# A planner that writes the issue order gets new costs, waits and port rules

## Chip, core and metric

The kernel runs on one core of one Trainium2 chip. The metric is the device time of one execution in microseconds (us). Five instruction streams work side by side on the core: TensorE (PE, matrix products), VectorE (DVE), ScalarE (ACT), GpSimd (POOL) and SyncE (SP, which here only issues DMA transfers). Each stream is worked off in the order in which it was written; an instruction that has to wait holds up everything behind it in its stream.

## The reference, cut to what matters

```python
kv  = einsum('bhsd,bhse->bhde', k, v)             # 4 batches, 8 heads, 576 tokens, 64 wide
x   = einsum('bhsd,bhde->bhse', q, kv)
x   = x / sqrt(mean(x*x, -1) + 1e-6) * g_norm     # -> 2304 tokens x 512
h   = x @ w_in                                    # 512 x 2048
y   = (h * tanh(softplus(h))) @ w_out             # 2048 x 512
h2  = y @ w2_in                                   # 512 x 1024
s   = h2 * softmax(h2)
out = layer_norm(s) * g_ln @ w2_out               # 1024 x 512
```

## The kernel before

The 2304 tokens stand in six blocks of 384 (b = 0 to 5), each with three tiles of 128 rows (r = 0 to 2). Every product is made of fp16 parts, a high and a low one, in three passes. The float data come as 64-bit words that the core decodes itself: one **piece** of a weight matrix (512 KB, 48 pieces: `("1", 0..15)` of w_in, `("2", 0..15)` of w_out, then `"3"` and `"4"` of the second layer) is loaded into one of five staging slots (`ld`, SP), scaled (`sc`, ACT, L598), has its sign taken out (`sg`, POOL, L603), is put together (`low`, `put`, DVE, L608 and L615) and split into high and low (`whi`, ACT, L626; `wlo`, DVE, L633 or L635). A slot is free for the fifth next piece when `put` is through.

The stages on TensorE are: k^T v of a batch (`kv`, L307); queries times that (`xo`, L482, in block 0 L352); `H`, the first product of the first layer (L738, units of 12 matmuls; L833 from block 3 on); `Y`, the second (L907, units of 12); the first product of the second layer (`"2"`, L1012, seven products for each pair of token tiles p = 0 to 8) and its second (`O`, L1148, likewise seven products of 12 matmuls).

Between `xo` and `H` a tile goes through `sq` (ACT), `ms` (DVE), `rho` (POOL, a power: L507 and L509), `xf` (DVE, L515), `xhi` (ACT), `xlo` (DVE); blocks 0 and 1 are then transposed on TensorE (`xP`, L460), the others by a DMA (`xT`, L539). Queries of blocks 2 to 5 come by `ldq` (SP, L281, into one buffer, so the next block's load waits until the last one's queries are used), `qhi`, `qlo`, and a transposing DMA `qT` (L434; three buffers, so each waits for the `xo` of the tile three before it). Queries of blocks 0 and 1 are transposed on TensorE (`qT`, L338 and L442).

A softmax tile of the second layer goes `ex` (ACT, L1049), `z` (DVE, L1055), `sq2` (ACT, L1060), `den` and `pw` (POOL, L1066 to L1076), `ln` (ACT, L1082), then `hi` (ACT, L1118), `lo` (DVE, L1124), and a transposing DMA (L1129). Out of the `O` bank, `e1`, `e2`, `e7` (ACT, L1159) keep partial products, `c12` (ACT, L1172) and `c11`, `c22`, `c21` (DVE, L1167) make the output rows.

None of this order is written out. Each step is a task with an engine, a cost in us, what it comes after, and a lag. `Plan.order` (list scheduling by due times) lays the tasks out, `Plan.search` tries 300 random changes of due times and keeps the order whose last TensorE task ends first; that order is then emitted. Where the plan leaves a gap on TensorE, the emitting loop puts dummy products (`keep_warm`, L1663, `idle<-ident` or `hp<-ident`), one for each 0.12 us of the gap less a constant:

```python
            if not heated and gap > 1.0:
                keep_warm(int((gap - 0.4) / 0.12), warm)
            elif gap > 0.5 and at_time < 150 and done.issuperset(h_free[h_line[0]]):
                keep_warm(int((gap - 0.2) / 0.12), h_open(h_line[0]))
```

The dummies read `ident`, which GpSimd writes at the start (L1676, L1677) beside two clears of buffers (L1681, L1682).

Of the kernel before, what the change touches and what calls it, by code (L numbers as in the profile page):

```python
# [142 lines left out]
def tile_attn_moe_moe2(  # L143
# [1036 lines left out]
    def task(key, engine, cost, fn, args, after=(), lag=0.1, due=None):  # L1180
# [9 lines left out]
    LAND, PAIR, QLD, PIECE = 2.0, 2.15, 3.0, 1.6  # L1190
# [3 lines left out]
    def far_group(kind, j):  # L1194
# [5 lines left out]
        for w, which in enumerate("rt"):  # L1200
            if w:
                for n in range(4):
                    after = [los["r", m] for m in range(parts[0])] if n == 0 else []
# [4 lines left out]
            for n in range(parts[w]):  # L1208
# [14 lines left out]
    for n, u in enumerate(PIECES):  # L1223
# [27 lines left out]
        task(("wlo", u), "V", 0.77 if scaled else 0.72, w_lo, (u,), [("whi", u)])  # L1251
# [23 lines left out]
    for b in range(B):  # L1275
        for i in range(4):
# [7 lines left out]
            task(("ld", b, i), "S", PAIR, load_pair, (b, i), free, LAND)  # L1284
# [10 lines left out]
    for c in range(4):  # L1295
        task(("lq0", c), "S", QLD / 4, load_q0, (c,), (), LAND)
# [441 lines left out]
```

## Time and profile before

| | |
|---|---|
| time, median of 3 runs (lowest, highest) | 594.47 us (593.57, 595.64) |
| profiled execution: time, span from first to last instruction | 594.5 us, 592.6 us |
| TensorE busy, matmuls | 581.6 us, 98% of the span, 4818 |
| VectorE, ScalarE, GpSimd busy | 428.3, 369.6, 138.7 us |
| DMA moved | 82.30 MB, mean 139 GB/s |
| chain that ended last: TensorE, DMA, ScalarE | 88%, 6%, 3% |

The span is what the trace covers; the time is that of the same execution as the runs measure it. A busy TensorE may be busy with dummies, which the page does not tell apart from work.

### The profile page before, as it was taken

The page shows a single profiled execution, that of the slowest core. Times are in us where ns is not written, and L with a number is a line of the kernel's source. Part 1 is how long each engine was busy: PE and PEld are TensorE (multiplying, and loading weights), DVE is VectorE, ACT ScalarE, POOL GpSimd, SP SyncE. Part 2 cuts the span into 40 slices and gives each one's busy share as a digit, 9 for nine tenths or more (in the row PEclk, how much of TensorE's full clock was granted, in tenths as well). Part 3 has the DMA queues.
Part 4 walks back from the last instruction along what each step waited for, and adds up shares of the span by engine and source line. Part 5 has one row for each costly group of instructions (what it writes and reads, how often), then busy time and mean ns, then how long its engine had stood idle before and what let it go on. Part 6 is the DMA issues. An engine that isn't in the chain of part 4 may idle for free.

```text
span 592.6 us, 12017 instructions
## 1 busy us (share of the span) xinstructions
PE 581.6 (98%) x4818; PEld 405.2 (68%) x4818; DVE 428.3 (72%) x722; ACT 369.6 (62%) x633; POOL 138.7 (23%) x180
## 2 busy tenths in 40 slices
PE   8899998999999999999999999999999999999997
PEld 6676665666666667877877778775455567767786
DVE  1587777887556858898775787887666888778751
ACT  4568555773646544455556765765767768888651
POOL 1526443320412530000100010000433115253300
PEclk9899999999999999999999999999999999999999
DMA  8982884997775440001342632607063329977695
GB/s 292 306 274 72 215 195 96 279 240 213 180 167 127 71 54 2 1 19 72 106 127 76 199 127 80 234 1 283 1 125 58 68 51 211 177 151 137 119 207 141
DMA packets 128423, 82.30 MB, mean 139 GB/s; under 512 B 94320, under 2 KB 115824, under 8 KB 128368
## 3 DMA queue, kind: packets, MB, share of 16 engines
q1 hardware_dynamic: 128208, 81.55, 54.9%
q8 instruction: 37, 0.61, 0.4%
q14 instruction: 18, 0.15, 0.1%
q10 hardware_dynamic: 160, 0.00, 0.0%
HBM read 46.67 MB, written 12.06 MB: 99 GB/s over the span
## 4 chain that ended last, share of the span: by engine, by line
PE 88%; DMA 6%; ACT 3%; DVE 1%; issue 1%; POOL 1%; SPq 0%; POOLq 0%; ACTq 0%
PE y L907 29%; PE hp L833 14%; PE h L1012 14%; PE op L1148 13%; PE hp L738 13%; DMA qraw<-in_q_dram 3%; PE kvp L307 2%; PE xo L482 1%; DMA st<-in_moe_w_in_dram 1%; DMA st<-in_moe_w_out_dram 1%; PE qTp L442 1%; PE qTp L338 1%; ACT g L884 1%; ACT w L626 0%; ACT qhl L421 0%
## 5 line engine op out<-in xcount | busy, mean ns | idle before, releaser
L907 PE MATMUL y<-g,w 128*128 128x384 f16 x1152 | 201.5, 326 | 1.5 <-ACT yT L927 1.5
L907 PEld LDWEIGHTS <-w 128*128 128x128 f16 x1152 | 110.9, 98 | 69.3 <-issue 1.6
L603 POOL TENSOR_SCALAR st<-st 128x512 f32<-128x512 f32 x48 | 39.0, 822 | 233.1 <-ACT P L598 231.4
L1148 PEld LDWEIGHTS <-w 128*128 128x128 f16 x756 | 74.0, 98 | 14.1 <-issue 1.5
L738 PEld LDWEIGHTS <-w 128*128 128x128 f16 x576 | 55.4, 98 | 36.8 <-issue 1.1
L1148 PE MATMUL op<-yT,w 128*128 128x256 f16 x567 | 72.2, 273 | 1.3 <-ACT g L1159 1.3
L738 PE MATMUL hp<-xT,w 128*128 128x384 f16 x384 | 66.7, 326 | 0.0
L889 DVE SCALAR_TENSOR_TENSOR g<-m,g 128x768 f16<-128x768 f32 x48 | 46.2, 972 | 12.1 <-ACT g L884 12.0
L833 PEld LDWEIGHTS <-ws 128*128 128x128 f16 x576 | 48.3, 98 | 3.0
L598 ACT ACTIVATE P<-st 128x512 f32<-128x512 f32 x48 | 32.0, 674 | 23.9 <-DMA st<-in_moe_w_in_dram 14.8
L608 DVE SCALAR_TENSOR_TENSOR st<-st 128x512 int32<-128x512 int32 x48 | 35.0, 734 | 16.3 <-POOL st L603 16.3
L877 ACT ACTIVATE m<-hp 128x384 f32<-128x384 f32 x48 | 23.1, 488 | 28.5 <-PE hp L738 27.3
L884 ACT ACTIVATE g<-m 128x768 f16<-128x768 f32 x48 | 39.7, 837 | 1.0 <-PE y L907 0.5
L833 PEld LDWEIGHTS <-w 128*128 128x128 f16 x432 | 36.6, 98 | 3.4
L1066 POOL TENSOR_SCALAR small<-small 128x1 f32<-128x1 f32 x18 | 15.5, 859 | 97.1 <-ACT e L1049 96.7
L872 ACT ACTIVATE m<-m 128x384 f32<-128x384 f32 (+1 forms) x24 | 16.4, 683 | 32.6 <-DVE m L859 32.5
L1012 PE MATMUL h<-st,w 128*128 128x512 f16 x150 | 35.3, 379 | 0.0
L1012 PEld LDWEIGHTS <-w 128*128 128x128 f16 x210 | 20.5, 98 | 21.6
L615 DVE SCALAR_TENSOR_TENSOR P<-P,st 128x512 int32<-128x512 int32 x48 | 33.4, 705 | 0.6
L738 PE MATMUL hp<-yT,w 128*128 128x384 f16 x192 | 32.5, 326 | 0.1
L1148 PE MATMUL op<-ws,w 128*128 128x256 f16 x189 | 30.9, 273 | 0.0
L1012 PEld LDWEIGHTS <-ws 128*128 128x128 f16 x168 | 16.5, 98 | 18.1
(173 smaller groups left out, 972.4 us busy)
## 6 DMA issues: line engine op xcount, KB each, us to landing
st<-in_moe_w_in_dram SPq DMA_DIRECT2D x24, 512.0 KB, 5.4
st<-in_moe_w_out_dram SPq DMA_DIRECT2D x24, 512.0 KB, 4.3
yT<-in_k_dram SPq DMA_DIRECT2D x16, 288.0 KB, 5.4
yT<-in_v_dram SPq DMA_DIRECT2D x16, 288.0 KB, 5.9
out_dram<-yT SPq DMA_DIRECT2D x18, 256.0 KB, 2.5
w_far<-F SPq DMA_DIRECT2D x15, 256.0 KB, 2.5
w_far<-st SPq DMA_DIRECT2D x11, 256.0 KB, 2.4
yT<-w_far SPq DMA_DIRECT2D x3, 896.0 KB, 8.2
```

Source lines behind the costliest of these rows:

```text
L598: nc.scalar.activation(out=P, in_=v[:, :, 1], func=ACTF.Copy, scale=2.0 ** -111)
L603: nc.gpsimd.tensor_scalar(out=v[:, :, 1], in0=v[:, :, 1], scalar1=0.0, scalar2=1.0, op0=ALU.mult, op1=ALU.mult)
L608: nc.vector.scalar_tensor_tensor(out=v[:, :, 0], in0=v[:, :, 0], scalar=29, in1=v[:, :, 1], op0=ALU.logical_shift_right, op1=ALU.bitwise_or)
L615: nc.vector.scalar_tensor_tensor(out=P.bitcast(I32), in0=P.bitcast(I32), scalar=3, in1=v[:, :, 0], op0=ALU.logical_shift_left, op1=ALU.bit ...
L738: nc.tensor.matmul(out=h_t[b, grp, i], lhsT=w1[:, f, c, wa], rhs=xT_t[b][:, C * xa + c], start=(c == 0 and m == 0), stop=(c == C - 1 and m ...
L833: nc.tensor.matmul(out=p[:, HT * fs:HT * fs + HT], lhsT=lhsT, rhs=x[:, C * xa + 2 * kx + c, HT * n:HT * n + HT], start=(opens and fs == 0 ...
L877: nc.scalar.activation(out=m_t[b, grp, i // 2][:, i % 2], in_=h_t.pop((b, grp, i)), func=ACTF.Mish, scale=2.0 ** -16)
L884: nc.scalar.activation(out=g_t[b, grp][:, 0, 2 * i:2 * i + 2], in_=m_t[b, grp, i], func=ACTF.Copy, scale=64.0)
L889: nc.vector.scalar_tensor_tensor(out=g_t[b, grp][:, 1, j], in0=m_t.pop((b, grp, i)), scalar=64.0, in1=g_t[b, grp][:, 0, j], op0=ALU.mult, ...
L907: nc.tensor.matmul(out=y_t[cc][:, 0:BLK], lhsT=w2[:, grp * G + ii, wa, cc * 128:(cc + 1) * 128], rhs=g_t[b, grp][:, ga, ii], start=(first ...
L1012: nc.tensor.matmul(out=T[p, "2" + bank], lhsT=yF[p][:, x, ya, c], rhs=w3[w][:, c, wa], start=(first and m == 0), stop=(m == 5), skip_group ...
L1148: nc.tensor.matmul(out=T[p, bank][:, 0:HB], lhsT=lnTs[p % 2][:, 8 * x + 4 * la + kk], rhs=w4[kk][:, 7 * HB * wa + HB * w:7 * HB * wa + HB ...
```

## The change

No operation is added, removed or altered. The planner's picture of the chip is: costs of most tasks (vector, scalar and GpSimd steps, query loads, k and v loads), the lag that stands by default between two engines (0.1 to 0.035), how early an engine can take its next task (`TAIL`), when each starts (`BEGIN`), and a rule by which GpSimd tasks wait while vector tasks of certain kinds run, in place of one shared counter. The core of it, with the load times and one of the cost lines:

```diff
-SHARED = {"low", "put", "wlo", "sg", "qlo", "xlo", "glo", "pow", "rho", "ylo"}
+FROM_BANK = 0
+TAIL = {"V": 0.085, "A": 0.105, "G": 0.05}
+BEGIN = {"S": 0.9, "P": 0.7, "V": 0.7, "A": 0.7, "G": 0.7}
+PORT = {"V": {"fS", "fL", "low", "put", "wlo", "qlo", "xlo", "glo", "cx", "cw", "xf", "ys", "yl", "z",
+              "sum", "lo", "qf"},
+        "G": {"sg", "qf"}, "g": {"rho", "den", "pw", "pow"}}
...
-    def add(self, key, engine, cost, fn, after=(), lag=0.1, due=None):
+    def add(self, key, engine, cost, fn, after=(), lag=0.035, due=None):
...
-            at, e = min((max(free[e], min(ready[k] for k in ks)), e)
-                        for e, ks in open_.items() if ks)
+            at, _, e = min((max(free[e], min(ready[k] for k in ks)), e != "V", e)
+                           for e, ks in open_.items() if ks)
             k = min((k for k in open_[e] if ready[k] <= at + 1e-9), key=lambda k: (k[0] not in self.first, due[k], index[k]))
+            if e == "G" and port[k] and held > at + 1e-9:
+                ready[k] = held
+                continue
             open_[e].remove(k)
-
-            if k[0] in SHARED:
-                at = max(at, port - 0.06)
-                port = at + tasks[k][1] - 0.12
+            if e == "V" and port[k]:
+                at = max(at, small)
             end = at + tasks[k][1]
-            free[e] = end
+            free[e] = end - TAIL.get(e, 0.0)
+            if port[k] and e == "V":
+                held = free[e]
+            elif port[k]:
+                small = free[e] if port[k] == 1 else at + 0.1
...
-    LAND, PAIR, QLD, PIECE = 2.0, 2.15, 3.0, 1.6
+    LAND, PAIR, PIECE = 2.0, 1.6, 1.49
+    QLD = {1: 4.2, 2: 2.35, 3: 2.35, 4: 3.6, 5: 2.6}
...
-            task(("pw", t), "G", 2.0, s_rho, (t,), [("sq2", t), ("den", t)])
+            task(("pw", t), "G", 1.4, s_rho, (t,), [("sq2", t), ("den", t)])
```

So the new order is what counts. The dummies of `keep_warm` change with the planned gaps: 27 `idle<-ident` instead of 13 at the start (19 ahead of the first `qT` and 8 behind it, instead of 7 and 6), and 4 `hp<-ident` ahead of `Y(1,0,0)` instead of 15 around the `xP` of block 1 (9 ahead of the last two `xP`, 4 and 2 behind them). On TensorE `H(0,1,0)` and two of the three-matmul quarters of the first `H` units now stand ahead of the last `xo` of block 1, and the three `xo` of block 2 move to earlier places, the first of them ahead of `H(1,0,0)`.

Three places in the order. First GpSimd, the start of the program: `ident` is what the dummies and the first transposes read, `kvf` and `kvr0` are the cleared buffers. Before:

```order
L1676 MEMSET ident_66 128x128
L1677 ISA
L1677 AFFINE_SELECT ident_66<-ident_66 128x128
L1681 MEMSET kvf_115 128x512
L1682 MEMSET kvr0_95 128x1024
```

And now:

```order
L1697 MEMSET kvf_115 128x512
L1698 MEMSET kvr0_95 128x1024
L1692 MEMSET ident_66 128x128
L1693 ISA
L1693 AFFINE_SELECT ident_66<-ident_66 128x128
```

The two clears have moved ahead of `ident`.

Second SP, the queue of transfers while the pieces of w_in 8 to 15 are loaded (`st`): `qraw` is a load of queries, `qT<-qhl` the transposing DMA of queries, `yT<-xhl` the one of block 2's `xT`. Before:

```order
L281 DMA qraw_1000<-in_q_dram 128x8x192
L551 DMA st_83<-in_moe_w_in_dram 128x4x256 x4
L539 DMA_TRANSPOSE yT_106<-xhl_1044 128x8x128
L539 DMA_TRANSPOSE yT_106<-xhl_1179 128x8x128
L551 DMA st_83<-in_moe_w_in_dram 128x4x256
L539 DMA_TRANSPOSE yT_106<-xhl_1255 128x8x128
```

And now:

```order
L449 DMA_TRANSPOSE qT_988<-qhl_965 128x8x128
L554 DMA_TRANSPOSE yT_106<-xhl_1010 128x8x128
L566 DMA st_83<-in_moe_w_in_dram 128x4x256
L449 DMA_TRANSPOSE qT_1068<-qhl_1007 128x8x128
L296 DMA qraw_1085<-in_q_dram 64x8x192 x2
L566 DMA st_83<-in_moe_w_in_dram 128x4x256 x2
L449 DMA_TRANSPOSE qT_1167<-qhl_1013 128x8x128
L554 DMA_TRANSPOSE yT_106<-xhl_1134 128x8x128
L566 DMA st_83<-in_moe_w_in_dram 128x4x256 x3
L554 DMA_TRANSPOSE yT_106<-xhl_1224 128x8x128
```

The three transposes of block 3's queries (`qT_988`, `qT_1068`, `qT_1167`) and the load of block 4's now stand among the weight loads; before they came after the load of w_out 12. `qT_1068` and `qT_1167` wait for the `xo` of block 2's second and third tile, and the loads behind them with them.

Third ACT near the end, from the `ex` of tile 16 (L1049, now L1064) to the `ln` of tile 16 (L1082, now L1097); the other L1082 or L1097 is the `ln` of tile 17, the first L1159 or L1174 behind it is `e1` of pair 6, whose result the third product `O(6,6)` waits for. Before:

```order
L1049 ACTIVATE e_4839,small_6208<-Q_6207,small_6208 128x1024
L1172 ACTIVATE yT_106<-op_6211 128x256
L1082 ACTIVATE Q_6207<-Q_6207,small_6245 128x1024
L1159 ACTIVATE g_91<-op_6353 128x256
L1060 ACTIVATE e_4839,small_6208<-Q_6207,small_6208 128x1024
L1118 ACTIVATE ws_2665<-Q_6207 128x512
L1159 ACTIVATE g_91<-op_6353 128x256
L1159 ACTIVATE g_91<-op_6403 128x256
L1082 ACTIVATE Q_6207<-Q_6207,small_6208 128x1024
```

And now:

```order
L1064 ACTIVATE e_4832,small_6204<-Q_6203,small_6204 128x1024
L1097 ACTIVATE Q_6203<-Q_6203,small_6237 128x1024
L1075 ACTIVATE e_4832,small_6204<-Q_6203,small_6204 128x1024
L1187 ACTIVATE yT_106<-op_6249 128x256
L1133 ACTIVATE ws_2639<-Q_6203 128x512
L1174 ACTIVATE g_91<-op_6362 128x256
L1097 ACTIVATE Q_6203<-Q_6203,small_6204 128x1024
```

Between the `ln` of tile 17 and `e1` there now stand `sq2` of tile 16, `c12` and a `hi`. On TensorE two more `O` products stand behind the last product of `"2"` than before (28 instead of 26).

## Rows read from the trace of the kernel before

**Rows 1.** Windows: us, busy time (instructions) of each engine, granted clock, DMA share, GB/s.
```profile
24.87:27.85 2.98, 2.98 (x29) 2.81 (x29) 0.42 (x1) 0.00 (x0) 0.12 (x1) 0.55 1.07 370
24.87:56.65 31.78, 31.75 (x409) 23.15 (x410) 23.59 (x38) 22.20 (x42) 12.64 (x16) 0.96 0.65 217
56.65:91.48 34.83, 33.37 (x230) 20.78 (x228) 25.68 (x39) 21.43 (x39) 14.57 (x13) 1.00 0.75 174
91.48:562.20 470.72, 470.62 (x3688) 323.85 (x3688) 359.28 (x603) 301.74 (x507) 99.07 (x132) 1.00 0.49 121
```

**Rows 2.** Who TensorE waited for: us in total, times, longest us.
```profile
PE qTp L442 <- DMA qraw<-in_q_dram: 1.7, 1, 1.7
PE y L907 <- ACT yT L927: 1.5, 1, 1.5
PE idle L1663 <- POOL ident L1677: 1.3, 1, 1.3
PE op L1148 <- ACT g L1159: 1.3, 1, 1.3
PE rT L363 <- ACT sq L357: 1.0, 1, 1.0
```

**Rows 3.** Timeline of TensorE, first 60 us: start, us, instruction, [idle before <-releaser].
```profile
1.34 1.67 PE L1663 MATMUL idle<-ident 128*128 128x256 f16 x7 [1.34 <-POOL ident L1677]
...
10.54 0.88 PE L338 MATMUL qTp<-ident,qraw 128*64 128x128 f32 x12
...
24.87 1.97 PE L442 MATMUL qTp<-ident,qraw 128*64 128x128 f32 x16 [1.67 <-DMA qraw<-in_q_dram]
...
29.63 1.09 PE L442 MATMUL qTp<-ident,qraw 128*64 128x128 f32 x16
```

**Rows 4.** Timeline of GpSimd at the start.
```profile
1.00 0.29 POOL L1677 TENSOR_SCALAR_AFFINE_SELECT ident<-ident 128x128 f32<-128x128 f32 x1
1.24 0.52 POOL L1681 MEMSET kvf<- 128x512 f32 x1
1.70 0.95 POOL L1682 MEMSET kvr<- 128x1024 f16 x1
```

**Rows 5.** The chain that ended last, 10 to 26 us: start, us, what.
```profile
11.45 0.75 SPq L281
...
12.25 12.48 DMA qraw<-in_q_dram
```

**Rows 6.** Timeline of TensorE around the dummies of block 1.
```profile
43.14 0.87 PE L482 MATMUL xo<-kvr,qT 128*64 128x128 f16 x24
...
52.19 1.15 PE L1663 MATMUL hp<-ident 128*128 128x256 f16 x9
...
54.04 0.60 PE L1663 MATMUL hp<-ident 128*128 128x256 f16 x4
```

**Rows 7.** Timeline of VectorE: the last `xf` of block 1.
```profile
51.34 0.69 DVE L515 SCALAR_TENSOR_TENSOR xf<-xo,rho 128x512 f32<-128x512 f32 x1 [0.61 <-POOL rho L509]
```

**Rows 8.** The chain of the whole span: one `Y` unit of 12 matmuls.
```profile
117.25 1.95 PE y L907 x12
```

**Rows 9.** Line L434: the query transposes on SP, duration in ns (min/median/max).
```profile
L434 SPq DMA_TRANSPOSE qT<-qhl x12: 1231/1236/2877, 59.8 to 191.9; - x12
```

**Rows 10.** DMA issues of the page: count, KB each, median us to landing.
```profile
st<-in_moe_w_in_dram SPq DMA_DIRECT2D x24, 512.0 KB, 5.4
```

**Rows 11.** Timeline of ScalarE ahead of the wait at 91.48.
```profile
88.36 0.68 ACT L598 ACTIVATE P<-st 128x512 f32<-128x512 f32 x1 [0.79 <-DMA st<-in_moe_w_in_dram]
...
90.93 0.88 ACT L927 ACTIVATE yT<-y 128x384 f32<-128x384 f32 x2
```

**Rows 12.** Timelines of GpSimd, VectorE and ScalarE (one row each) around the last stall.
```profile
559.92 2.41 POOL L1076 TENSOR_SCALAR small<-small 128x1 f32<-128x1 f32 x1
...
561.07 1.21 DVE L1124 TENSOR_TENSOR g<-Q,g 128x1024 f16<-128x1024 f32 x1
...
562.37 1.24 ACT L1082 ACTIVATE Q<-Q,small 128x1024 f32<-128x1024 f32 x1 [1.92 <-POOL small L1076]
```

More of the change, by code (lines that the diff above doesn't have):

```diff
@@ L56, in prepare @@
         self.index = {k: n for n, k in enumerate(tasks)}
+        self.port = {}
+        for k, t in tasks.items():
+            bank = t[0] == "V" and k[0] in ("xf", "xlo") and k[1] < (3 if k[0] == "xf" else FROM_BANK)
+            self.port[k] = 0 if bank else 1 if k[0] in PORT.get(t[0], ()) else 2 if (
+                t[0] == "G" and k[0] in PORT["g"]) else 0
         edges = {k: [(a, tasks[a][4]) for a in t[3]] + [(a, 0.0) for a in self.behind.get(k, ())]
@@ L82, in order @@
     def order(self, due):
-        tasks, index = self.tasks, self.index
+        tasks, index, port = self.tasks, self.index, self.port
         waits = dict(self.count)
         ready = {k: 0.0 for k in tasks}
-        free, open_, port = {}, {}, 0.0
+        free, open_, held, small = {}, {}, 0.0, 0.0
         for k, t in tasks.items():
-            free.setdefault(t[0], 0.0)
+            free.setdefault(t[0], BEGIN.get(t[0], 0.0))
             open_.setdefault(t[0], [])
@@ L1177, in o_out, with task @@
         nc.sync.dma_start(out=outv[n // R, n % R], in_=osb(p, t))
-    def task(key, engine, cost, fn, args, after=(), lag=0.1, due=None):
+    def task(key, engine, cost, fn, args, after=(), lag=0.035, due=None):
         add(key, engine, cost, lambda: fn(*args), after, lag, due)
@@ L1231, in tile_attn_moe_moe2 @@
         task(("ld", u), "S", PIECE, w_load, (u,), before + [opened], LAND)
-        task(("sc", u), "A", 0.66, w_scale, (u,),
+        task(("sc", u), "A", 0.675, w_scale, (u,),
              [("ld", u)] + ([("wlo", PIECES[n - NDEC])] if n >= NDEC else []))
-        task(("sg", u), "G", 0.7, w_sign, (u,), [("ld", u), ("sc", u)])
-        task(("low", u), "V", 0.72, w_low, (u,), [("sg", u)])
-        task(("put", u), "V", 0.72, w_put, (u,), [("low", u), ("sc", u)])
+        task(("sg", u), "G", 0.67, w_sign, (u,), [("ld", u), ("sc", u)])
+        task(("low", u), "V", 0.69, w_low, (u,), [("sg", u)])
+        task(("put", u), "V", 0.69, w_put, (u,), [("low", u), ("sc", u)])
         if u[0] == "4":
@@ L1283, in tile_attn_moe_moe2 @@
                 free = [("kv", 3, i - 2) if i > 1 else ("kv", 2, i + 2), ("put", ("2", 15))]
-            task(("ld", b, i), "S", PAIR, load_pair, (b, i), free, LAND)
+            task(("ld", b, i), "S", PAIR if b or i else 2.4, load_pair, (b, i), free, LAND)
     for b in range(B):
         for i in range(4):
-            task(("kv", b, i), "P", 1.27 if b in WIDE else 0.92, kv_pair, (b, i),
+            task(("kv", b, i), "P", 1.27 if b in WIDE else 0.95, kv_pair, (b, i),
                  [("ld", b, i), ("kv", b, i - 1) if i else None], 0.25)
@@ L1295, in tile_attn_moe_moe2 @@
     for c in range(4):
-        task(("lq0", c), "S", QLD / 4, load_q0, (c,), (), LAND)
+        task(("lq0", c), "S", 0.6 if c else 1.3, load_q0, (c,), (), LAND)
     for c in range(4):
@@ L1316, in tile_attn_moe_moe2 @@
         task(("xhi", *u), "A", 0.5, e_xhi, u, [("xf", *u)])
-        task(("xlo", *u), "V", 0.55, e_xlo, u, [("xhi", *u)])
+        task(("xlo", *u), "V", 0.69, e_xlo, u, [("xhi", *u)])
     tiles = [(b, r) for b in range(1, NB) for r in range(R)]
@@ L1322, in tile_attn_moe_moe2 @@
             ("qT", 0, c) for c in range(4)]
-        task(("ldq", b), "S", QLD, load_q, (b,), free, LAND)
+        task(("ldq", b), "S", QLD[b], load_q, (b,), free, LAND)
     bank_a = {}
@@ L1358, in tile_attn_moe_moe2 @@
         task(("ms", *u), "V", 0.68, a_ms, u, [("sq", *u)] + ring("ms", 3, ("rho", *u)))
-        task(("rho", *u), "G", 2.4 if b >= NI else 2.0, a_rho, u, [("ms", *u)] + ring("rho", 3, ("xf", *u)))
+        task(("rho", *u), "G", 1.95, a_rho, u, [("ms", *u)] + ring("rho", 3, ("xf", *u)))
         task(("xf", *u), "V", 0.69, a_xf, u,
@@ L1364, in tile_attn_moe_moe2 @@
             task(("xhi", *u), "A", 0.62, t_xhi, u, [("xP", *u)])
-            task(("xlo", *u), "V", 0.7, t_xlo, u, [("xhi", *u)])
+            task(("xlo", *u), "V", 0.69, t_xlo, u, [("xhi", *u)])
             task(("xT", *u), "-", 0.0, lambda: None, (), [("xlo", *u)])
@@ L1368, in tile_attn_moe_moe2 @@
         task(("xhi", *u), "A", 0.62, a_xhi, u, [("xf", *u)] + ring("xhl", 2, ("xT", *u)))
-        task(("xlo", *u), "V", 0.7, a_xlo, u, [("xhi", *u)])
+        task(("xlo", *u), "V", 0.69, a_xlo, u, [("xhi", *u)])
         gone = [("kv", 0, 3)] if b == 2 else [("H", 0, 3, i) for i in range(G)] if b == 3 else [
```

62 lines of the change are left out of this document (31 added, 31 removed).

## The prediction

> **What bounds the kernel now.** I read the busy shares first, then who TensorE waited for, then the windows by stage, and only then single timelines. TensorE is busy for 470.62 of the 470.72 us between 91.48 and 562.20 [rows 1], 79% of the span, at the full granted clock (1.00, 2.4 GHz), and no dummy stands there before the change. No order can make that stretch shorter while no operation changes; it can only let it begin earlier, or spoil it. What an order can win lies outside: the five longest waits, 6.8 us together [rows 2], and the dummies, which the page counts as busy. The first of the waits is not the order's to take away as long as nothing lands earlier: the transposes of block 1's queries (L442) start when their load lands, at 24.73 [rows 5], and everything behind follows from that. So I count from 24.87 [rows 3], where TensorE takes them up.
>
> **The start.** GpSimd's two clears now stand ahead of `ident`. They took from 1.24 to 2.65 [rows 4], so `ident` comes about 1.4 us later, at 2.7, and 19 dummies stand there instead of 7. Seven took 1.67 us with their modelled ends, which is 0.21 a dummy [rows 3], so the first transpose waits until 2.7 + 19 x 0.21 = 6.7 instead of 3.3. The 8 dummies behind it are 2 more, 0.2 to 0.4. At full clock a dummy costs 0.11 (9 took 1.15 [rows 6]); whether the clock has risen by then decides how much of the delay is won back, since work that ran at 1.2 GHz before then runs at 2.4. I put the last query transpose of block 0 at 13.3, against 10.54 + 0.8 = 11.34 before [rows 3]; 15.0 if the clock rises late. That one frees the buffer into which block 1's queries are loaded: SP issued that load at 11.45 [rows 5]. It then took 12.48 us to land, where the weight loads take 5.4 in the median [rows 10], so it queued behind transfers issued earlier. My choice is that a load issued 2 us later lands 0.3 us later, because the work ahead of it in the queues is the same; the bounds are 0 and the whole 2.0 (3.6 with the late clock). TensorE has room for its own part: it stood idle for 1.7 us before 24.87, and for 1.0 at L363 [rows 2]. Term: **+0.3**.
>
> **Block 1.** Right after the landing the granted clock was 0.55 in the mean [rows 1], that is at its lower level of 1.2 GHz for most of 3 us, after the two idle times just named: 16 transposes took 1.97 us, later ones of the same shape 1.09 [rows 3]. With the later start TensorE has little idle time left before 24.87, so I expect the clock not to fall, 0.9 us. Against it stand `H(0,1,0)`, 1.95 us [rows 8], and two quarters of 0.49 in front of the last `xo` of block 1. That ended at 44.0 [rows 6], and now ends at 44.0 + 2.9 - 0.9 = 46.0. From there to the last `xf` it was 7.3 us (51.34 [rows 7]), but much of that was GpSimd working off the powers of the first two tiles; the first `xo` now comes 1.5 places' work earlier, so I keep 51.3 for the last `xf`. The bound on the bad side is 46.0 + 7.3 = 53.3, on the good side 50.5. Before, TensorE did not take that tile up at 52.0: nine dummies ran until 53.3, and six more followed, four of them in [rows 6]. Now it goes on at once: last `xP` until 52.5, `H(0,1,3)` until 54.5, `xo` of block 2 (0.67) until 55.1. `H(1,0,0)` therefore starts at 55.1, where it started at 56.65 without that `xo`; in equal work the order is 56.65 + 0.67 - 55.1 = 2.2 us ahead (0.2 with the bad bound, 3.0 with the good one). For this the transposed queries of block 2 must be in by 54.4, which I expect but with less than 2 us to spare.
>
> **The wait at Y(1,0,0).** From `H(1,0,0)` on 16 units and two more `xo` remain, 32.5 us (16 x 1.95 [rows 8] and 1.3), so TensorE comes to `Y(1,0,0)` at 87.6. Its banks must be emptied by ScalarE first. Before, that was late by 1.5 us [rows 2], since ScalarE stood behind a weight load that landed at 88.3 [rows 11]. In the new order ScalarE meets the same thing: the scaling of piece 14 stands ahead of the bank copies. On SP the load of that piece is queued behind a query transpose that waits for the third `xo` of block 2, which ends at 79.8 (24.7 us of work behind 55.1), and behind one `xT`. So 79.9, two transposes of 1.24 [rows 9], the issue at 82.4, landing 5.4 later [rows 10] at 87.8, then scaling, a split and a copy of 0.4 to 0.7 each [rows 11]: the bank is free at 89.5 and `Y(1,0,0)` starts at 89.6 instead of 91.48. The wait thus stays, 2.0 us long, with another cause ahead of it. Term: **-1.9** (with the +0.3 of the start, which moves all of it). If the load lands in time, -3.9; if block 1 takes the bad bound, nothing is won here. Behind it the transposes of block 2 must land before `H(2,0,0)`, which now comes 7.8 us of `Y` work earlier; xo at 79.8 plus the chain of sq, ms, rho, xf, xhi, xlo and xT, 10 us at least, against 93.5. I take it as covered; a late one costs its lateness one for one.
>
> **From there to 562.** VectorE has 359.28 of 470.72 us there [rows 1], so a start 1.6 us earlier asks nothing of it that it cannot give. Price if a vector chain were the cover that breaks: each late bank its own lateness. I take 0.
>
> **The last stall.** At 562.20 TensorE waited 1.3 us [rows 2] for `e1` of pair 6. ScalarE had reached it late, because the `ln` ahead of it waited 1.92 us for a GpSimd instruction on 128 numbers that lasted 2.41 us, until the vector instruction that began at 561.07 was through [rows 12]. In the new order the products of `"2"` end two `O` products earlier (1.31 each), so that all of softmax has 2.6 us more before `O(6,6)`; but `sq2`, `c12` and `hi` (2.1 us together) come between `ln` and `e1`. That alone would win 0.5. The GpSimd instruction also meets only one long vector instruction (`z` of tile 16), because the `lo` behind it now waits for the `ln` itself: about 1 us less. Together 1.3 or a little less; I take **-1.0**, bounds 0 (the hold comes back in full) and -1.3.
> The Trainium skill (SBUF — State Buffer, Who interferes with whom) says that GpSimd and VectorE take a shared port in turn, and that the later one is blocked until the first instruction is through. By that GpSimd would have been free at the end of the first vector instruction, some 1.2 us earlier than [rows 12] show; the trace has it blocked through two in a row. By the rule the worst case of the new order would be shorter, and the sum 591.7 instead of 591.9.
>
> **Sum.** 594.5, the profiled execution's own time, + 0.3 - 1.9 - 1.0 = **591.9**. The profiled run is as good as the median (594.47), so this stands for both.
>
> **Rivals.** A difference of 0.3%, 1.8 us, is about what a measurement of this kernel can tell from none.
> *Both waits go away* (12%): piece 14 lands before 86.5 and the last stall is gone in full: 594.5 + 0.3 - 3.9 - 1.3 = 589.6. For it speaks that DMA had room (174 GB/s against 370 [rows 1]), against it the SP queue as worked out.
> *The landing follows the issue* (18%): block 1's queries come 2.0 later, and all behind them: 594.5 + 2.0 - 1.9 - 1.0 = 593.6, no difference. The late clock makes it 595.2.
> *The order buys nothing* (17%): `xf` takes the bad bound or the `xo` of block 2 holds TensorE up, so `Y(1,0,0)` starts at 91.5 again; with or without the last stall 593.5 to 594.8.
> *The SP queue turns against it* (13%, slower): the query transposes stand among the weight loads now, and wait for `xo` products that TensorE reaches only after units that need weights. Each us that piece 14 lands after 87.8 is a us at `Y(1,0,0)`. It decides from 10 us to landing on (92.4): then `Y(1,0,0)` starts at 94.3 and the kernel is 1.8 us slower even with the last stall won; at 12.48 us, as the query load took [rows 5], 598. Against it: 5.4 in the median [rows 10].
> The forecast itself has 40%, between 590.4 and 593.2.
>
> **Chances and range.** Faster by over 0.3% (under 592.7): the first rival and nearly all of the forecast, 0.51. Within 0.3%: the second and third and the rest, 0.35. Slower: 0.14. The range from 589.5 to 595.0 leaves out most of the last rival and a little at the lower end.
>
> **What would show it.** The first transposes of block 0 near 6.7 instead of 3.3, the load of block 1's queries issued near 13.4 and landing near 25; the granted clock staying at 1.00 between 24 and 28; `H(1,0,0)` near 55; a wait of 1 to 2 us before `Y(1,0,0)` near 89.6, with a weight load ahead of ScalarE; busy without a gap from there to the end; and no wait, or one under 0.5, at the sixth `O` pair. I am wrong if the load lands later than 26, if TensorE waits for the `xo` of block 2 or for `H(2,0,0)`, or if new waits show between 91 and 560.

## The result: 1.4% slower, and the profile after

The changed kernel takes 603.05 us (median of 6 runs, 600.38 to 606.34) where the kernel before takes 594.35 (6 runs, 592.49 to 596.67): a ratio of 1.0145, 95% interval 1.0104 to 1.0187. I had forecast 591.9. Its profiled execution is the fastest of its six, 600.38 us, 5.9 more than the profiled execution before.

The longest waits of TensorE after the change (us in total, times, longest), which answer to [rows 2]:

```profile
PE xo L497 <- DVE xf L530: 4.1, 1, 4.1
PE idle L1679 <- POOL ident L1693: 2.7, 1, 2.7
PE rT L378 <- ACT sq L372: 1.5, 1, 1.5
PE h L1027 <- ACT yT L1036: 1.1, 1, 1.1
PE op L1163 <- ACT g L1174: 0.5, 1, 0.5
```

The wait for the queries (1.7), for the bank at `Y(1,0,0)` (1.5) and the 1.3 of the last stall are gone. New is the first row: an `xo` that waits for VectorE's `xf`. The start, from the timeline of TensorE, answers to [rows 3]:

```profile
2.70 4.08 PE L1679 MATMUL idle<-ident 128*128 128x256 f16 x19 [2.70 <-POOL ident L1693]
...
12.35 0.88 PE L353 MATMUL qTp<-ident,qraw 128*64 128x128 f32 x12
...
25.56 1.09 PE L457 MATMUL qTp<-ident,qraw 128*64 128x128 f32 x16
```

Sixteen transposes of block 1 take 1.09 us where they took 1.97: the clock did not fall here. The new wait, on the same timeline:

```profile
77.93 2.11 PE L753 MATMUL hp<-xT,w 128*128 128x384 f16 x12
84.19 0.83 PE L497 MATMUL xo<-kvr,qT 128*128 128x128 f16 x12 [4.14 <-DVE xf L530]
84.85 3.79 PE L753 MATMUL hp<-xT,w 128*128 128x384 f16 x12
88.48 6.01 PE L922 MATMUL y<-g,w 128*128 128x384 f16 x36
94.33 0.60 PE L1679 MATMUL hp<-ident 128*128 128x256 f16 x4
94.77 4.06 PE L922 MATMUL y<-g,w 128*128 128x384 f16 x24
```

The row at 84.19 is `xo(2,2)`: its bank is the one that `xf(2,1)` must empty first. The unit behind it, `H(1,1,3)`, takes 3.63 us from start to start instead of 1.95. The window of that unit says why (granted clock, DMA share and GB/s stand last):

```profile
84.85:88.48 3.63, 3.63 (x15) 1.78 (x13) 3.54 (x6) 2.62 (x5) 1.41 (x2) 0.53 1.18 220
```

The clock had fallen to its lower level. One stall thus costs 4.3 + 1.7 us, and four dummies ahead of `Y(1,0,0)` 0.4. `Y(1,0,0)` starts at 94.77, 3.3 later than before (91.48 [rows 1]). The last matmul group starts 6.0 later (594.52 against 588.49). The 2.7 between come from a new wait for a load at 184 (0.7 with its tail) and from stalls in the second layer that were not there (3.4 in all; the largest 1.3 at 499 and 0.6 at 507), less the last stall of before with its tail (1.4). The wait at 184 stands in front of a product of keys and values, again on the timeline of TensorE:

```profile
184.21 0.92 PE L322 MATMUL kvp<-yT 96*64 96x64 f32 x24 [0.63 <-DMA yT<-in_v_dram]
```

The chain that ended last, through the 22 us ahead of the stall (start, us, what):

```profile
62.47 5.26 DMA qraw<-in_q_dram
...
67.75 0.63 ACT qhl L436
...
73.53 0.68 DVE P L630
...
74.97 4.19 DMA st<-in_moe_w_in_dram
...
79.27 0.68 ACT P L613
...
80.84 0.53 ACT w L641
...
82.16 0.10 DVE g L904
...
83.46 0.69 DVE xf L530
```

The timeline of ScalarE gives the two waits in it:

```profile
67.75 0.63 ACT L436 ACTIVATE qhl<-qraw 128x512 f16<-128x512 f32 x1 [3.28 <-DMA qraw<-in_q_dram]
...
79.27 0.68 ACT L613 ACTIVATE P<-st 128x512 f32<-128x512 f32 x1 [3.90 <-DMA st<-in_moe_w_in_dram]
```

ScalarE stood at the split of block 3's queries until they had landed, then at a scaling until that piece had landed; VectorE's `xf(2,1)` stood behind two splits and a `glo` that needed ScalarE. The engines in this stretch are simply fuller than before (windows of before, then of after; the order of the engines is that of [rows 1]):

```profile
60.00:97.00 37.00, 35.54 (x243) 22.05 (x241) 26.32 (x40) 21.22 (x40) 16.67 (x14) 1.00 0.73 169
```

```profile
60.00:97.00 37.00, 32.86 (x210) 19.93 (x208) 30.54 (x46) 22.99 (x43) 18.93 (x14) 0.95 0.94 214
```

VectorE has 30.5 us of 37 to do instead of 26.3, and the DMA share rose from 0.73 to 0.94. In the second layer ScalarE's waits for GpSimd's power steps at `ln` went from 2.8 us in 2 waits to this:

```profile
ACT Q L1097 <- POOL small L1091: 13.3, 10, 2.2
```

and one of them is the largest of the new stalls (timelines of GpSimd, ScalarE and TensorE):

```profile
495.25 1.66 POOL L1090 TENSOR_TENSOR small<-small,nhalf 128x1 f32<-128x1 f32 x1
497.01 1.82 POOL L1091 TENSOR_SCALAR small<-small 128x1 f32<-128x1 f32 x1
...
498.87 1.24 ACT L1097 ACTIVATE Q<-Q,small 128x1024 f32<-128x1024 f32 x1 [1.78 <-POOL small L1091]
500.01 0.58 ACT L1036 ACTIVATE yT<-h 128x512 f32<-128x512 f32 x1
...
500.64 1.67 PE L1027 MATMUL h<-st,ws 128*128 128x512 f16 x7 [1.13 <-ACT yT L1036]
```

The copy that empties the bank stands behind an `ln` that waits for GpSimd, and TensorE waits for the copy.

### The profile page after: what moved, and what is told of

Same layout as the page of the kernel before. It is cut to its first block, busy times and chain, and to the rows that moved or that the text cites. A ratio compares the mean times of both kernels' runs of the same rounds, so it can differ in the third digit from the quotient of the medians.

```text
span 598.6 us, 12042 instructions
## 1 busy us (share of the span) xinstructions
PE 583.4 (97%) x4821; PEld 404.4 (68%) x4821; DVE 427.1 (71%) x722; ACT 368.7 (62%) x633; POOL 140.4 (23%) x180
## 4 chain that ended last, share of the span: by engine, by line
PE 77%; DVE 7%; ACT 6%; issue 3%; DMA 3%; POOL 2%; SPq 0%; POOLq 0%; DVEq 0%; ACTq 0%
PE y L922 28%; PE hp L848 14%; PE hp L753 12%; PE op L1163 9%; PE h L1027 8%; PE kvp L322 2%; PE xo L497 1%; ACT e L1075 1%; DMA qraw<-in_q_dram 1%; PE idle L1679 1%; DVE st L623 1%; DMA qT<-qhl 1%; DMA yT<-in_v_dram 1%; DMA st<-in_moe_w_in_dram 1%; DVE g L1139 1%
## 5 line engine op out<-in xcount | busy, mean ns | idle before, releaser
L618 POOL TENSOR_SCALAR st<-st 128x512 f32<-128x512 f32 x48 | 45.7, 966 | 194.7 <-ACT P L613 172.6
L753 PEld LDWEIGHTS <-w 128*128 128x128 f16 x576 | 55.8, 99 | 36.9 <-issue 2.1
L753 PE MATMUL hp<-xT,w 128*128 128x384 f16 x384 | 69.1, 332 | 0.1
L904 DVE SCALAR_TENSOR_TENSOR g<-m,g 128x768 f16<-128x768 f32 x48 | 46.8, 993 | 12.2 <-ACT g L899 12.1
L1081 POOL TENSOR_SCALAR small<-small 128x1 f32<-128x1 f32 x18 | 12.9, 716 | 135.2 <-ACT e L1064 134.6
L753 PE MATMUL hp<-yT,w 128*128 128x384 f16 x192 | 33.2, 326 | 0.0
## 6 DMA issues: line engine op xcount, KB each, us to landing
st<-in_moe_w_in_dram SPq DMA_DIRECT2D x24, 512.0 KB, 5.0
st<-in_moe_w_out_dram SPq DMA_DIRECT2D x24, 512.0 KB, 4.2
```

What stands on the lines that cost most here:

```text
L618: nc.gpsimd.tensor_scalar(out=v[:, :, 1], in0=v[:, :, 1], scalar1=0.0, scalar2=1.0, op0=ALU.mult, op1=ALU.mult)
L753: nc.tensor.matmul(out=h_t[b, grp, i], lhsT=w1[:, f, c, wa], rhs=xT_t[b][:, C * xa + c], start=(c == 0 and m == 0), stop=(c == C - 1 and m ...
L904: nc.vector.scalar_tensor_tensor(out=g_t[b, grp][:, 1, j], in0=m_t.pop((b, grp, i)), scalar=64.0, in1=g_t[b, grp][:, 0, j], op0=ALU.mult, ...
```

## The experiments

Both orders can be written out as lists of tasks, `old` and `new`, and emitted without the planner. `upto(head, rest, last)` takes one list up to a task and what is left from the other; `move(order, tasks, behind)` moves tasks. Ratios are to the kernel before, with 95% intervals; the new order's is 1.0145. As a yardstick for the early loss I use the time from the start of `xo(2,0)` to that of `Y(1,0,0)`: 16 units of 1.95 and three `xo` of 0.67, 33.2 us of work. After the change it is 39.6, and in three other profiles with the same order there (early_new, short_pow, pw_2) 40.5 to 41.0.

### Where the loss lies

```diff
+order = upto(new, old, ("Y", 3, 0, 0))     # early_new
+order = upto(old, new, ("Y", 3, 0, 0))     # late_new
+order = upto(new, old, ("xo", 2, 0))       # start_new
```

> All engines in the new order up to Y(3,0,0) (about 263 us), from there on in the order of before. Theory A (two separate losses: the stall in front of xo(2,2) with the lower clock behind it, and ScalarE's order in the second layer): up to Y(1,0,0) 3.3 us are lost, 0.8 more near 180, nothing after that, and the last stall of 1.3 us comes back as before; 594.4 + 3.3 + 0.8 = 598.5. Rival B (one loss, all from the early part, which leaves the other engines behind so that the second layer stalls too): the stalls near 417, 469, 481, 499 and 507 us show here as well, 601 to 602.

> The order of before up to Y(3,0,0), from there on the new order. Theory A: the second layer brings its own stalls (0.4 + 0.2 + 0.3 + 1.3 + 0.6 and 0.6 in smaller ones, 3.4 us) and wins the last one (1.3): 594.4 + 2.1 = 596.5. Rival B: without the early part's delay no new stall shows, and only the last one goes: 593.1.

> The new order up to the first xo of block 2 alone (54 us), from there on the order of before. My prediction's second step says that TensorE is 1.4 us ahead at H(1,0,0) in the new order, and that what held Y(1,0,0) up before (ScalarE behind a weight load) does not move: no gain at Y(1,0,0), a longer wait there, 594.0 to 594.8. If that wait was tied to TensorE's own work ahead of it, the lead goes through: 593.0. If the loads that the start puts off cost more than the lead (rival: the start did it), it is slower: 596 and more.

early_new: 1.0093 (1.0057 to 1.0129); the stall at `xo(2,2)` is there (4.4), the second layer's stalls are not, the last stall is back (1.3). late_new: 1.0086 (1.0055 to 1.0117); the second layer's stalls are all there, the last one gone. The seam costs it 1.6 us at 277 us, where the two orders meet, so its own loss is nearer 3.5 than 5.1. Two separate losses, then, as theory A had it: each list shows its own stalls and not the other's. Their sizes were more than theory A counted: the medians are 601.8 and 600.4 us where it forecast 598.5 and 596.5, and by its time alone early_new would fit rival B; the places of the stalls decide between them. start_new: 0.9980 (0.9954 to 1.0005), no harm and no clear gain. The loss begins behind 54 us.

### The second layer

```diff
+order = upto(old, new, ("Y", 3, 0, 0))     # late_fixed
+order = move(order, [("ex", 1), ("z", 1)], ("k1", 1))
+order = move(order, [("hi", 2, "c")], ("k2", 4))
+order = move(order, [("yh", 8, "c"), ("yl", 8, "c"), ("yh", 8, "d")], ("k1", 5))
+order = move(order, [("ln", 9)], ("k7", 5))
+order = move(order, [("hi", 4, "a"), ("hi", 4, "s")], ("e2", 2))
```

> As late_new, but at five places ScalarE takes a copy out of a TensorE bank ahead of the step that stood before it and waited: k1(1) ahead of ex(1), k2(4) ahead of hi(2,c), k1(5) ahead of two splits of the second layer's weights, k7(5) ahead of ln(9), e2(2) ahead of hi(4,a) and hi(4,s). Theory A says that the banks were late only by their place behind those steps: 2.8 of the 3.4 us go, 594.4 + 2.1 - 2.8 = 593.7. Rival (ScalarE has no room there, so what is moved behind the copies stalls the products later): no better than late_new, 596.5.

1.0093 (1.0060 to 1.0127), no better than late_new. The stalls that were aimed at went, others came at 426.7 (1.7), 488.5 (0.9) and 512.0 (1.1), and ScalarE's waits for GpSimd stayed at 13.2 us. Theory A's claim that the place of the copies is the cause falls here, and the rival, that `ln` waits for GpSimd, holds. Moving the copies does not help while `ln` waits.

```diff
-        nc.gpsimd.tensor_scalar(out=var, in0=T[t, "sq"], ..., op0=ALU.mult, op1=ALU.add)
-        nc.gpsimd.tensor_tensor(out=rs, in0=var, in1=nhalf[:, 0], op=ALU.pow)
-        nc.gpsimd.tensor_scalar(out=small(t, "bz"), in0=T[t, "sz"], scalar1=rs, ...)
+        nc.gpsimd.tensor_tensor(out=rs, in0=T[t, "sq"], in1=nhalf[:, 0], op=ALU.pow)
```

> The new order, but the three GpSimd instructions between sq2 and ln of the second layer's softmax are one: the scaling ahead of the power and the product behind it are left out (ln takes another number as its bias). Theory E (ScalarE stands at ln, 13.3 us in 10 waits against 2.8 in 2 before, because GpSimd's small instructions are held up; the bank copies behind ln make TensorE wait): the ten waits fall below 5 us in all, and the stalls near 499 and 507 us (1.3 and 0.6) go: 1.5 to 2 us less than the new order, 601. Rival F (the second layer stalls because ScalarE has too much ahead of the copies, whatever ln waits for, as late_fixed's stalls that turned up at other places suggest): the stalls stay, 603.

The kernel leaves out the scaling ahead of the power and the product behind it. 1.0090 (1.0056 to 1.0123). The waits fell to 2.7 us, and the stalls near 499 and 507 are gone; 1.2 us of the 3.4 remain. That is theory E; the stalls show it, while the interval in time still touches the new order's. Which number of the plan put `ln` there:

```diff
-            task(("pw", t), "G", 1.4, s_rho, (t,), [("sq2", t), ("den", t)])
+            task(("pw", t), "G", 2.0, s_rho, (t,), [("sq2", t), ("den", t)])
```

> The changed kernel with one number of the planner as before: pw costs 2.0 us, not 1.4. Its order is the same as the new one up to 415 us. Theory E (that cost put each ln ahead of the moment at which GpSimd is through): ScalarE's waits for GpSimd fall from 13.3 to under 6 us, and the second layer's stalls from 3.4 to under 1.5 us: 600.5 to 601.5 against 603 of the new order. Rival: the order of the second layer changes in other ways, and other stalls take the place: 603.

1.0106 (1.0079 to 1.0132). ScalarE's waits:

```profile
ACT Q L1097 <- POOL small L1091: 3.5, 4, 1.5
```

With one cost as it was before, nearly 10 of the 13.3 us go, and about half of the second layer's stalls in its profile (to 1.6 us, with 0.5 more at 588). The gain in time, 1.0106 against 1.0145, is of the size expected, but the two intervals overlap.

### The early loss

```diff
+order = move(new, [("qhi", 3, 0), ("qlo", 3, 0), ("qT", 3, 0)], ("sc", ("2", 7)))   # qhi_later
+order = move(order, [("qlo", 3, 0), ("qT", 3, 0)], ("glo", 1, 0, 1))
...
+order = move(new, [("xo", 2, 2), ("qT", 3, 2), ("sq", 2, 2), ("ms", 2, 2)], ("Y", 0, 1, 1))   # xo_late
...
+dummies[("xo", 2, 2)] = 30                # warm_xo, order = new
```

> The new order, but the first split of block 3's queries (qhi(3,0) on ScalarE, qlo(3,0) on VectorE) stands a few steps later: behind mi(1,0,3), whi(2,4), ghi(1,0,1) and the scaling of w_out 7 on ScalarE, behind xf(2,0) and glo(1,0,1) on VectorE. Theory A (ScalarE stood 3.28 us at that split until the queries had landed, and the pieces, xf(2,0) and with them xf(2,1) slipped by as much): xf(2,0) comes some 3 us earlier, the next weight load too, and the stall of 4.1 us in front of xo(2,2) falls to 1 us or less, with no lower clock behind it: 4 to 5 us less than the new order, 598 to 599. Rival C (the loads themselves are late, since the DMA share is 0.94 there; what lands late stays late): the stall stays within 1 us of 4.1, 602 to 603.

> The new order, but xo(2,2) stands two units later on TensorE, behind Y(0,1,1), with its sq and the query transpose that waits for it moved along. Theory A (everything that feeds block 2 is late, and TensorE only meets it first at xo(2,2)): xo(2,2) comes at about 85 as before, now without a wait; the time goes to Y(1,0,0), whose banks ScalarE cleared at 95.0, or to H(2,0,0), which needs the transpose of tile 2, landed at 97 to 98: 0 to 2 us are won, 601 to 603. Rival D (one product stands in the wrong place, the rest is in time): the 4.1 us and the 1.7 at the lower clock are won: 597 to 598.

> The new order, with 30 dummies (3.3 us) on TensorE ahead of xo(2,2), into the bank that H(1,1,3) takes next. They can begin when ScalarE has emptied that bank, at 80.8, so most of the stall is filled. Theory A: the wait for xf(2,1) is as long as before, but the granted clock does not fall behind it: H(1,1,3) takes 1.95 instead of 3.63 us, 1.7 us less than the new order, 601.4. If the lower clock has another cause than the idle time, H(1,1,3) stays at 3.6 and the time at 603.

qhi_later: 1.0105 (1.0071 to 1.0139), which overlaps with the new order's interval; stall 3.9, yardstick 39.9. Theory A had named the wrong wait: `xf(2,0)` did come 2.5 us earlier, but ScalarE then stood 2.2 us for w_out 7, which landed 5.9 us behind its issue, and the rest was as before. Taking one wait for a load out of ScalarE's stream put it at the next load.

xo_late: 1.0172 (1.0143 to 1.0201), no faster than the new order (slower by the median, but the intervals overlap); yardstick 41.8. The stall shrank to 0.9, and the timeline shows it again at `Y(1,0,0)`, with the low clock behind it (6.3 us for two units):

```profile
84.93 0.83 PE L497 MATMUL xo<-kvr,qT 128*128 128x128 f16 x12 [0.86 <-DVE xf L530]
...
97.09 6.49 PE L922 MATMUL y<-g,w 128*128 128x384 f16 x24 [6.99 <-ACT yT L942]
```

ScalarE's copies stood behind three scalings; in the chain one weight load, issued behind the early load of block 4's queries, took 9.37 us to land. Rival D falls: it is not one misplaced product. It gave back none of the 0 to 2 us that theory A counted on.

warm_xo: 1.0124 (1.0081 to 1.0168), yardstick 40.6.

```profile
83.01 3.44 PE L1679 MATMUL hp<-ident 128*128 128x256 f16 x30
88.33 0.83 PE L497 MATMUL xo<-kvr,qT 128*128 128x128 f16 x12 [1.89 <-DVE xf L530]
89.00 2.11 PE L753 MATMUL hp<-xT,w 128*128 128x384 f16 x12
```

`H(1,1,3)` takes 1.95: with dummies in most of the wait the clock did not fall behind it. The 1.7 us did not come back in time, though. `xo(2,2)` started 30.4 us behind `xo(2,0)` where it was 29.05 after the change, and `Y(1,0,0)` waited 1.1 for ScalarE, where it had waited for nothing.

```diff
+            n = C // 2 if f >= 8 else C          # w_in: rows 0 to 128 n of the piece only
+            n = 512 if 2 <= f < 8 else 1024      # w_out: columns 0 to n only
```

> The new order, but the fourteen weight loads that are issued between 40 and 95 us (pieces 2 to 7 of w_out, 8 to 15 of w_in) bring only the first half of their 512 KB; the second half keeps what the slot held. All other steps stay. Theory G (what slips ahead of xo(2,2) is the landing of loads, 4 to 6 us from issue where the plan counts 3.5, with a DMA share of 0.94): they land 1 to 2 us sooner, each wait of ScalarE for them shrinks, the stall in front of xo(2,2) falls below 1.5 us with little or no lower clock behind it, Y(1,0,0) starts at 89 to 91 instead of 94.8: 598 to 599. Rival J (GpSimd is the late one: signs and powers held up between vector instructions, 5.26 us for one sign at 55.9 and 4.0 for the two steps of rho(2,1)): the stall stays above 3 us, 602 to 603.

> The order of before with the same half loads, as the control. Theory G: the wait of 1.5 us at Y(1,0,0), where ScalarE stood behind a weight load, goes, and nothing else changes: 593. If the old order gains as much as the new one (4 us or more), the loads are not what sets the two apart.

half_new: 1.0086 (1.0055 to 1.0117), stall 2.9, yardstick 38.2; the DMA share in 60 to 97 us fell from 0.94 to 0.71. half_old: 0.9955 (0.9932 to 0.9978). Between the two orders there is still 1.3%, so the bytes of the weights are not what sets them apart, and theory G falls as the main cause as far as weights go. The loads of queries were left whole. In half_new the weight loads landed in 3.1 us in the median (5.0 after the change), but block 3's queries took 5.4 and ScalarE still stood 3.2 us for them, and two pieces behind block 4's queries took 6.0 and 6.2. How much of the stall hangs on the query loads no run here tells: qhi_later took ScalarE's wait for them away, and the stall stayed.

```diff
+order = move(new, [("wlo", ("2", 7)), ("wlo", ("2", 6)), ("glo", 1, 1, 0)], ("xf", 2, 1))   # xf_first, xf_rho
...
-        nc.gpsimd.tensor_scalar(out=ms, in0=ms, scalar1=1e-6, scalar2=1.0, ...)              # xf_rho alone
```

> The new order, but xf(2,1) stands ahead of the splits of w_out 7 and 6 and of glo(1,1,0) on VectorE, which wait for ScalarE. rho(2,1) was ready at 80.8, so xf(2,1) runs until 81.5, and the stall in front of xo(2,2) is 1.7 instead of 4.1 us; if the clock does not fall after so short a wait, 1.7 more are won. Theory A (everything around it is late, the wait moves on): Y(1,0,0) then waits for ScalarE's copies, at 93 to 95: 601 to 602.5. Rival D (VectorE's order alone): 599.

> As xf_first, and the first of the two GpSimd steps of each rho (adding 1e-6) is left out. That step took 2.4 us for 8 numbers per row at 76.7, where the same step took 0.6 at 87.0. Theory J (GpSimd is held up by VectorE): rho(2,1) is ready at 78.5, xf(2,1) runs right behind the two puts, until 79.7, and xo(2,2) no longer waits. With theory A the time then stands at Y(1,0,0): 600 to 602. If xf_rho is no better than xf_first, GpSimd was no part of it.

xf_first: 1.0173 (1.0144 to 1.0203), yardstick 40.2; xf_rho: 1.0178 (1.0149 to 1.0208), 41.1. Neither is faster than the new order; both are slower by the median, with intervals that overlap. In xf_first the stall halves, no low clock follows, and the wait moves on to `Y(1,0,0)`, as theory A said, with more in it than it said:

```profile
85.49 0.83 PE L497 MATMUL xo<-kvr,qT 128*128 128x128 f16 x12 [1.90 <-DVE xf L530]
86.16 2.11 PE L753 MATMUL hp<-xT,w 128*128 128x384 f16 x12
...
98.92 1.55 PE L922 MATMUL y<-g,w 128*128 128x384 f16 x7 [4.36 <-ACT yT L942]
```

In xf_rho, which leaves out the step ahead of the power, GpSimd has one instruction instead of two, and is through 3.9 us behind the end of `ms`, 0.3 sooner than in xf_first (timelines of GpSimd and VectorE):

```profile
81.31 3.83 POOL L522 TENSOR_TENSOR rho<-ms,nhalf 128x8 f32<-128x8 f32 x1 [3.62 <-DVE ms L517]
...
81.15 1.28 DVE L621 SCALAR_TENSOR_TENSOR st<-st 128x512 int32<-128x512 int32 x2
82.35 1.28 DVE L628 SCALAR_TENSOR_TENSOR P<-P,st 128x512 int32<-128x512 int32 x2
85.17 0.69 DVE L528 SCALAR_TENSOR_TENSOR xf<-xo,rho 128x512 f32<-128x512 f32 x1 [1.54 <-POOL rho L522]
```

The power, 1.65 us where it runs behind another GpSimd step, took 3.83: it began 0.16 us after the first of four vector instructions in a row and ended 1.5 us after the last. Theory J is right in that VectorE holds GpSimd, and wrong in its price: nearly all of the step left out was time that GpSimd would have waited anyway.

### Durations as measured

```diff
-        task(("ld", u), "S", PIECE, w_load, (u,), before + [opened], LAND)
+        task(("ld", u), "S", PIECE, w_load, (u,), before + [opened], LAND + 1.5)
-        task(("ldq", b), "S", QLD[b], load_q, (b,), free, LAND)
+        task(("ldq", b), "S", QLD[b], load_q, (b,), free, LAND + 1.0)
-        task(("rho", *u), "G", 1.95, a_rho, ...)
+        task(("rho", *u), "G", 3.0, a_rho, ...)
-            task(("pw", t), "G", 1.4, s_rho, ...)
+            task(("pw", t), "G", 2.5, s_rho, ...)
```

All four are plan_measured, the first two plan_loads, the last two plan_gpsimd.

> The changed kernel with four durations as the traces show them: a weight piece lands 1.5 us later in the plan (5.0 from issue), a load of queries 1.0 later (5.3), rho of blocks 1 to 5 costs 3.0 (1.95), pw 2.5 (1.4). Its plan puts xo(2,2) 3 us later on TensorE and ends 0.8 us later. Theory A with E (the order was planned with durations that are too short, and so without slack): the stall in front of xo(2,2) is below 1.5 us, the second layer's stalls below 1 us: 595 to 597, no slower than before. Rival: the tight order as such is the trouble (blocks 2 and 3 pulled forward into a stretch where VectorE, GpSimd and the DMA queues are nearly full), and better numbers do not help: 600 and more.

> The changed kernel with the loads' landings as measured (a weight piece 1.5 us later in the plan, a load of queries 1.0 later), rho and pw as in the change. If the loads are what the early loss hangs on: no stall above 1.5 us between 60 and 100 us; the second layer keeps its stalls (ScalarE waits 10 us or more for GpSimd): 596 to 598. If GpSimd's steps are: a stall of 3 us or more in front of an xo of block 2 or of Y(1,0,0) stays, 600 to 603.

> The changed kernel with rho at 3.0 and pw at 2.5 us, the loads as in the change. The second layer's stalls are below 1 us in any case. If the early loss hangs on GpSimd's steps: no stall above 1.5 us between 60 and 100 us, 593 to 595. If it hangs on the loads: a stall of 3 us or more stays there, 598 to 601.

plan_measured: 0.9967 (0.9946 to 0.9988), with a DMA share of 0.98 and 32.8 us of VectorE in the 37 from 60 to 97 us. So a full stretch is not the trouble as such. That it is faster than the kernel before is not shown: its runs had a mean granted clock of 0.997 to 1.000, the runs of before beside it 0.991 to 1.000, and the two of those at 1.000 took 592.8 us, no more than its own 593.8. Yardstick 36.0; what is left there:

```profile
82.37 0.83 PE L497 MATMUL xo<-kvr,qT 128*128 128x128 f16 x12
...
90.28 6.01 PE L922 MATMUL y<-g,w 128*128 128x384 f16 x36 [0.79 <-ACT yT L942]
```

ScalarE waits 0.4 us for GpSimd in the whole second layer. plan_loads: 1.0106 (1.0086 to 1.0127), yardstick 37.7 with 2.9 us of wait at `Y(1,0,0)`, and 13.3 us of waits for GpSimd. plan_gpsimd: 1.0116 (1.0087 to 1.0145), yardstick 37.8 (one more `H` unit in it taken off), 3.1 at `Y(1,0,0)`, 0.4 for GpSimd. In both no `xo` of block 2 waits more than 0.3 us, and the wait stands at `Y(1,0,0)`. For the second layer the three plans form a series: with pw at 1.4 the waits are 13.3, at 2.0 3.5, at 2.5 0.4. For the early part neither pair alone is enough. But each plan is another order in thousands of places, and 5.0 of plan_gpsimd's 7.7 us against plan_measured lie ahead of `H(1,0,0)`, where its clock was 0.72; which durations the early loss hangs on stays open. Each of these plans is also the outcome of one search from one random seed; no run used another, so part of plan_measured's good order could be luck of that search, which is not tested.

### The parts that did no harm

```diff
+order = move(old, [("ln", 17)], ("e1", 6))                            # tail_fix
...
+order = move(upto(new, old, ("xo", 2, 0)), [("ln", 17)], ("e1", 6))   # start_tail
```

> The order of before with one move: e1 of pair 6 stands ahead of the ln of tile 17 on ScalarE, where ln waited 1.92 us for GpSimd. My prediction's last step, alone: the last stall of 1.3 us goes, ln begins as late as before, 0.2% faster, 593.8 against 595.1. Rival: the stall moves to the next O product, because ScalarE has as much to do as before: no difference.

> The new order up to the first xo of block 2, the order of before behind it, and the same move of e1: the two parts of the new order that did no harm. start_new measured 0.998 of before (interval 0.9954 to 1.0005); with the last stall gone 0.996, 592.5 to 593. Rival: start_new's 0.998 was chance, 0.998 to 1.000.

tail_fix: 0.9982 (0.9962 to 1.0002), in time not told from no change; the stall itself is 0.3 instead of 1.3. start_tail: 0.9938 (0.9917 to 0.9958), 591.87 us: the fastest version here, faster than both kernels. The last stall, in start_tail, which answers to [rows 2]:

```profile
563.80 1.14 PE L1163 MATMUL op<-yT,w 128*128 128x256 f16 x9 [0.31 <-ACT g L1174]
```

## Why the prediction was wrong, by its own steps

**The start** was right in the profiled execution: `ident` and the dummies at 2.70, the last query transpose until 13.15 (I said 13.3), the next load issued at 13.26 (13.4). The landing came at 24.90, 0.2 later (I took 0.3); the transposes began 0.7 later, at 25.56, since TensorE was still at other work behind a wait of 1.5 us for ScalarE. Over the twelve profiles that have the new start up to `xo(2,0)`, though, block 1's transposes begin at 25.3 to 25.7 in six and at 26.5 to 26.8 in six. My rival "the landing follows the issue" does not come out of that. The load landed at 24.7 to 25.1 in the early six and at 25.5 to 26.4 in the late six, but in only one of the late ones (warm_xo, 0.35 us) did TensorE wait for it; in the others the transposes stand behind a part of an `H` unit that ran at the lower clock.

**Block 1**: the clock stayed at 1.00, the last `xo` ended at 46.3 (46.0), `H(1,0,0)` started at 55.8 (55.1). Right, and 0.7 short. But in the six late profiles the mean clock from 24 to 36 us is 0.72 to 0.86, and `xo(2,0)` starts at 57.9 to 59.0 instead of 55.1 to 55.8, as in this window of xf_first:

```profile
24.00:36.00 12.00, 11.44 (x163) 9.19 (x163) 9.06 (x18) 4.96 (x10) 4.28 (x3) 0.72 0.87 292
```

The new start is not needed for it: in the same stretch the clock was 0.86 in the profile of before and in late_fixed and 0.72 in half_old, all with the old start, and 1.00 in late_new and tail_fix. Whole runs spread with it under both orders: after the change a mean clock of 0.997 goes with 600.4 to 602.4 us and 0.992 to 0.994 with 603.7 to 606.3; the runs of before beside early_new go from 592.2 at 0.999 to 600.0 at 0.990. What lowers the clock in one execution and not in the next stays open. It is a likely part of what the median lost beyond the profiled 5.9 us.

**The wait at Y(1,0,0)** is the step that failed. I counted "16 units and two more `xo`", 32.5 us, as work without a wait, and let `xo(2,2)` end at 79.8. TensorE was there at 79.9, but `xf(2,1)` ended at 84.1, 12.1 us after `xo(2,1)`. I checked the third `xo` for what is queued behind it, not for the bank that it needs. 0.7 (late at `H(1,0,0)`) + 4.3 + 1.7 (low clock) + 0.4 (dummies) less the 2.0 of a wait that did not come make 5.1 us, from my 89.6 to 94.77. Two of the signs that I had named for being wrong came true with it: TensorE waits for an `xo` of block 2, and new waits stand between 91 and 560. Behind it stood my fourth rival, the SP queue: piece 14 was issued at 88.46 behind two transposes, 6 us later than counted because `xo(2,2)` came late, and its scaling began at 92.72, past the 92.4 from which that rival decides; the copies ended at 95.5. The load itself took 4.2, less than the 5.4 counted, so its lateness is that of `xo(2,2)`. That the queue would have held `Y(1,0,0)` up with `xo(2,2)` on time is not shown; in xo_late the wait did move there. The price of that rival has a slip: by its own rule 12.48 us to landing give 598.8, not 598.

**From there to 562** I took 0; it was 0.7 at 184 and 3.4 in the second layer, where ScalarE's waits for GpSimd went from 2.8 to 13.3 us. I looked only at how busy VectorE is. The cost line `pw` 1.4 was in my own extract of the diff, and [rows 12] show a GpSimd step of 2.41 us; I used the row for the last stall alone, not for the other `ln`.

**The last stall** was right: I took 1.0; 1.3 is gone in the changed kernel, and 1.0 in tail_fix and start_tail.

## What to carry to other kernels

A planner's durations set not only an order but its slack: with numbers that were too short by 1 to 2 us engines here stood at instructions whose data had not landed, and what waited in order passed its lateness on. In such a stretch single moves only send the wait on (qhi_later, xo_late, warm_xo and xf_first moved it, none removed it); what took the loss away here was a plan with durations as measured under load (one plan, plan_measured), or the old order where the new one has no slack (start_tail). In a forecast, every instruction that is moved forward needs its own check of what frees its buffer, on the fullest engine's stream; "busy without a gap" is no row of the new order.

## What was not expected of the hardware

GpSimd was held through a row of vector instructions, not one: 3.83 us for one power in xf_rho (above), 5.26 for one sign at 55.87 in the new order. The Trainium skill (SBUF — State Buffer, Who interferes with whom) says that whoever issues first has the shared ports for the whole instruction, and the other is blocked. By that GpSimd's turn would come after the first of the four; the trace disagrees, as [rows 12] did, and the measurement decides.

TensorE's clock fell behind the waits of 4.1, 4.4 and 7.0 us and cost 1.7, 1.7 and 2.4 us on top of them. It fell behind 2.9 in plan_loads (0.56 in the 6.8 us behind it) and not behind 3.1 in plan_gpsimd (1.00 in the 3.9 us behind it):

```profile
93.27 6.99 PE L922 MATMUL y<-g,w 128*128 128x384 f16 x24 [2.90 <-ACT yT L942]
```

```profile
97.06 4.06 PE L922 MATMUL y<-g,w 128*128 128x384 f16 x24 [3.11 <-ACT yT L942]
```

Behind 1.9 us (xf_first, warm_xo) it did not fall, though it had before behind 1.67 [rows 3]. The length of the wait alone does not decide.
